# Key-value sums of a second attention layer as bursts on two column halves of the array, with a head-half layout and the last tile in halves

## The chip, the cores and the metric

The kernel runs on one core of a Trainium2 chip. The metric is the device time of the core in microseconds (us), from many executions; most of them agree within 0.3%. The profiled span of one execution is about 1.7 us shorter than its device time. All runs quoted are fast, at a granted TensorE clock of 0.995 to 1.000, unless the text says otherwise.

Ratios below are computed as the mean time of one kernel's fast runs over the mean time of the other kernel's fast runs of the same rounds, so they are not quite the ratio of the medians that stand beside them. The interval after a ratio is its 95% interval.

PE is TensorE, PEld its weight loads, DVE is VectorE, ACT is ScalarE, POOL is GpSimd, SP is SyncE. "num" means the numerator matmuls of the linear attention.

## The reference, cut to what matters

Four residual layers on 2048 tokens of width 512: linear attention with a learned feature map (A), gated ReLU unit (B), A again, B again, with the same weights both times.

```python
x = x + A(layernorm(x));  x = x + B(layernorm(x))
x = x + A(layernorm(x));  x = x + B(layernorm(x))

def A(x):                                   # 32 heads of width 16
    phi_q = [softmax(q @ w_phi), softmax(-q @ w_phi)]     # 2 x 16 features
    phi_k = [softmax(k @ w_phi), softmax(-k @ w_phi)]
    kv  = einsum("bhsf,bhsd->bhfd", phi_k, v)             # sum over all tokens
    z   = einsum("bhsf->bhf", phi_k)
    num = einsum("bhqf,bhfd->bhqd", phi_q, kv)
    den = einsum("bhqf,bhf->bhq", phi_q, z) + 1e-6
    return (num / den) @ wo

def B(x):
    return (relu(x @ W_gate) * (x @ W_up)) @ W_down       # inner width 1376
```

The sum over all tokens matters here: no numerator of the second attention layer can start before the last token tile (tile 15 of 16, 128 tokens each) has gone through its layer normalisation, its key projection, its softmax and its key-value sum.

## The kernel before

The program is emitted as a graph of operations, each with an engine, the buffers it reads and writes, and a planned duration in ns. A list scheduler then decides the order of the instructions on each engine, and the engines run those orders with semaphore waits between them. It tries 4 weights and 12 passes and keeps the order with the shortest planned span. So a changed duration or dependency anywhere can move instructions everywhere.

The parts that the change and the argument touch:

```python
# layer normalisation of one token tile (the "apply" is the last line)
op("dve", bn_stats(stats6[t] <- x_sb[t]));  op("dve", bn_aggr(mv[t] <- stats6[t]))
op("pool", rv1 = var + eps);                op("pool", rstd = rv1 ** -0.5)
op("dve", tensor_scalar(ytile[yb] <- (x_sb[t] - mean) * rstd))    # 128x512 bf16, planned 407 ns
dma_transpose(yT[t] <- ytile[yb])                                  # on the SP queue

# key normalisation of one tile
op("dve", tensor_reduce(Zk <- expk[t]))                            # planned 1215
op("dve", reciprocal(rZk <- Zk))                                   # planned 545
parts = [("pool", 0, 2)] if t < NT - 2 else [("pool", 0, 1), ("dve", 1, 2)]
for eng, s0, s1 in parts:
    op(eng, tensor_tensor(expk[t, s0:s1] <- expk[t, s0:s1] * rZk)) # planned 1930 on GpSimd

def kv_acc(self, t, tag):                   # 8 matmuls of 128x129 for each token tile
    for g in range(NG):
        s, c = g // 4, g % 4
        bank, j = g // 3, g % 3
        op("pe", matmul(pb[bank][:, j * 130:j * 130 + 129],
                        expk[t, s, c * 128:(c + 1) * 128],         # stationary, 128 columns
                        vsb[t, c, 0:129]), ...)                    # moving, 8 heads x 16, and ones
# ... kv_fin: two products on VectorE for each of three banks build the masked kvbd ...

# the turn from layer 1 (B) to layer 2 (A)
mix(steps_B(tiles(3)), steps_K(1) + steps_K(2) + [lambda: self.q_proj(0, mring, "A2")])
for t in range(12):
    self.kv_acc(t, "A2")
for f in steps_K(3):
    f()
for t in tiles(3):
    self.kv_acc(t, "A2")
self.kv_fin("A2")

def glu_down(self, t, ring, tag):           # 11 matmuls of 128x512, one residual, later one store
```

The softmax here doesn't subtract the row's maximum and nothing guards it: scores larger than these inputs give would overflow.

## Time and profile before

| | before |
|---|---|
| device time, median of 3 first runs | 394.07 us |
| profiled span | 392.7 us |
| PE busy / DVE busy / ACT busy / POOL busy | 96% / 68% / 53% / 42% |
| first numerator of layer 1 / of layer 2 | 54.84 / 241.10 us |
| first gate matmul of the last layer | 259.11 us |

The page of the kernel before, its busy times and its chain that ended last (shares of the span by engine):

```profile
PE 377.3 (96%) x2277; PEld 206.9 (53%) x2320; DVE 267.4 (68%) x554; ACT 207.1 (53%) x389; POOL 166.4 (42%) x272
...
PE 84%; DVE 5%; POOL 4%; DMA 2%; ACT 2%; issue 2%; SPq 0%; DVEq 0%; ACTq 0%; POOLq 0%
```

TensorE is busy nearly always, and the chain runs mostly along it. The next view is the chain between 216 and 245 us, which is the turn to layer 2; its first line gives shares by line of the program (L587 key and value projection, L633 key-value sums, L660 query projection, L752 down projection of layer 1).

```profile
by line: PE ps L587 31.8%; PE ps L633 20.8%; PE ps L660 19.9%; PE ps L752 17.0%; PE ps L676 5.3%; DVE kvbd L644 3.7%; DVE kvbd L649 0.8%; issue 0.8%
```

Here the chain is TensorE alone, down to the two VectorE products just before the numerators. The timeline of PE (start, duration, engine, line, operands, count, and in brackets the idle time before the group and what ended it):

```profile
236.16 1.36 PE L633 MATMUL ps<-vsb,expk 128*128 128x129 bf16 x21
237.36 1.03 PE L587 MATMUL ps<-wv_p,yT 128*128 128x512 bf16 x4
238.22 2.82 PE L633 MATMUL ps<-vsb,expk 128*128 128x129 bf16 x46
241.10 0.54 PE L676 MATMUL ps<-kvbd,expq 128*128 128x144 bf16 x6
```

The last 46 sums are a backlog: (2.82 - 0.22) / 45 = 58 ns each, without a hole. No bracket stands on any of these lines. GpSimd's last key product of tile 15 ended at 239.24. The line of that product in the kernel before:

```profile
237.74 1.50 POOL L604 TENSOR_TENSOR expk<-expk,rZk 128x512 bf16<-128x512 bf16 x1 [0.94 <-DVE rZk L601]
```

One more view of the kernel before is needed later: VectorE's layer-norm applies of tiles 12 to 15 of layer 2.

```profile
216.50 0.41 DVE L564 TENSOR_SCALAR ytile<-x_sb,mv,rstd 128x512 bf16<-128x512 bf16 x1
221.17 1.75 DVE L564 TENSOR_SCALAR ytile<-x_sb,mv,rstd 128x512 bf16<-128x512 bf16 x1
224.84 0.41 DVE L564 TENSOR_SCALAR ytile<-x_sb,mv,rstd 128x512 bf16<-128x512 bf16 x1
227.13 0.41 DVE L564 TENSOR_SCALAR ytile<-x_sb,mv,rstd 128x512 bf16<-128x512 bf16 x1 [1.06 <-POOL rstd L552]
```

The same instruction takes 0.41 us three times and 1.75 us once.

### The profile page before, as it was taken

Reading aid. Unit: us, or ns where it says so; the run is one execution under the profiler, and the core shown is the slowest. Engines: PE = TensorE matmul, PEld = TensorE weight load, DVE = VectorE, ACT = ScalarE, POOL = GpSimd, SP = SyncE. Lnnn points to the kernel's source line nnn. Section 1 sums busy time; section 2 is a strip of 40 time slices with the busy share of each in tenths; the row PEclk is TensorE's granted clock in tenths of the full one; section 3 lists DMA queues with packets and bytes.
Section 4 is the critical chain, followed back from the end, with each engine's and each line's share of the span. In section 5 each row is a group of like instructions: output and inputs, shape, how many; then the busy total and the mean of one; then the engine's idle time right before and its main releaser. Section 6 shows DMA issues by size and latency. Waiting matters only on the chain.

```text
span 392.7 us, 6311 instructions
## 1 busy us (share of the span) xinstructions
PE 377.3 (96%) x2277; PEld 206.9 (53%) x2320; DVE 267.4 (68%) x554; ACT 207.1 (53%) x389; POOL 166.4 (42%) x272
## 2 busy tenths in 40 slices
PE   5889999999999999999999999989999999999996
PEld 3445564677644444444444467467774454444442
DVE  4999878777757899857747867877875666222122
ACT  5898659744624413532553484975564462453350
POOL 5389945642623463363334552574444253000000
PEclk9999999999999999999999999999999999999999
DMA  6833672322211322401000110242323132100001
GB/s 182 220 69 79 200 276 43 67 53 43 42 40 27 43 53 46 85 7 29 13 13 2 27 29 2 48 61 53 76 54 61 27 56 53 42 14 13 15 27 53
DMA packets 61519, 23.01 MB, mean 59 GB/s; under 512 B 53456, under 2 KB 60464, under 8 KB 61488
## 3 DMA queue, kind: packets, MB, share of 16 engines
q1 hardware_dynamic: 60912, 22.08, 24.8%
q10 hardware_dynamic: 576, 0.52, 0.5%
q8 instruction: 18, 0.29, 0.3%
q14 instruction: 13, 0.11, 0.1%
HBM read 7.91 MB, written 2.10 MB: 25 GB/s over the span
## 4 chain that ended last, share of the span: by engine, by line
PE 84%; DVE 5%; POOL 4%; DMA 2%; ACT 2%; issue 2%; SPq 0%; DVEq 0%; ACTq 0%; POOLq 0%
PE ps L728 39%; PE ps L752 19%; PE ps L587 7%; PE ps L707 6%; PE ps L660 5%; PE ps L676 4%; POOL expk L604 3%; DVE stats L547 2%; PE ps L633 2%; PE ps L618 2%; DMA yT<-ytile 1%; DMA x_sb<-in_A_x_dram 1%; POOL rstd L552 1%; DVE ytile L564 1%; ACT expq L663 1%
## 5 line engine op out<-in xcount | busy, mean ns | idle before, releaser
L728 PE MATMUL ps<-yT,Wg 128*128 128x512 bf16 (+3 forms) x435 | 125.9, 336 | 2.0 <-ACT numbf L366 1.1
L728 PE MATMUL ps<-yT,Wu 128*128 128x512 bf16 (+3 forms) x436 | 124.2, 336 | 0.4
L730 ACT ACTIVATE gate_sb<-ps 128x512 bf16<-128x512 f32 (+3 forms) x110 | 56.2, 512 | 108.7 <-PE ps L728 103.2
L752 PE MATMUL ps<-Wd,hT 128*128 128x512 bf16 (+1 forms) x340 | 104.0, 379 | 0.6
L604 POOL TENSOR_TENSOR expk<-expk,rZk 128x1024 bf16<-128x1024 bf16 (+1 forms) x32 | 59.6, 1878 | 30.9 <-DVE rZk L601 21.6
L728 PEld LDWEIGHTS ps<-yT,Wg 128*128 128x128 bf16 (+1 forms) x440 | 43.7, 100 | 34.4 <-issue 1.5
L728 PEld LDWEIGHTS ps<-yT,Wu 128*128 128x128 bf16 (+1 forms) x440 | 43.7, 100 | 33.4 <-ACT expk L735 0.8
L752 PEld LDWEIGHTS ps<-Wd,hT 128*128 128x128 bf16 (+1 forms) x352 | 34.1, 98 | 37.3 <-DVE x_sb L754 0.7
L737 DVE TENSOR_TENSOR hT<-gate_sb,expk 128x512 bf16<-128x512 bf16 (+3 forms) x73 | 28.7, 393 | 31.0 <-ACT expk L735 30.2
L547 DVE BATCH_NORM_STATS2 stats<-x_sb 128x6 f32<-128x512 bf16 x64 | 42.1, 675 | 5.0 <-DMA x_sb<-in_A_x_dram 4.7
L599 DVE TENSOR_REDUCE Zk<-expk 128x64 f32<-128x1024 bf16 x32 | 38.0, 1197 | 10.1 <-ACT expk L590 8.4
L366 ACT ACTIVATE numbf<-ps 128x432 bf16<-128x432 f32 x64 | 32.9, 538 | 17.7 <-PE ps L676 17.4
L701 POOL TENSOR_TENSOR osb<-tsc 128x512 bf16<-128x512 bf16 x28 | 32.7, 1168 | 21.3 <-DVE tsc L696 18.2
L707 PE MATMUL ps<-wo_p,oT 128*128 128x512 bf16 x122 | 38.7, 379 | 0.2
L551 POOL TENSOR_SCALAR rv<-mv 128x1 f32<-128x1 f32 (+1 forms) x55 | 12.3, 229 | 61.0 <-DVE mv L548 60.8
L735 ACT ACTIVATE expk<-ps 128x512 bf16<-128x512 f32 (+3 forms) x73 | 36.2, 495 | 0.6 <-PE ps L728 0.4
L754 DVE TENSOR_TENSOR x_sb<-x_sb,ps 128x512 bf16<-128x512 bf16 x32 | 21.7, 682 | 20.8 <-PE ps L752 20.6
L663 ACT ACTIVATE expq<-ps 128x1024 bf16<-128x1024 f32 (+1 forms) x40 | 32.3, 865 | 6.1 <-PE ps L660 5.8
L676 PE MATMUL ps<-kvbd,expq 128*128 128x144 bf16 x256 | 34.6, 226 | 0.4 <-DVE kvbd L649 0.2
L660 PE MATMUL ps<-yT,Wqp 128*128 128x512 bf16 x121 | 33.6, 379 | 1.2 <-ACT expq L663 1.0
L740 DVE TENSOR_TENSOR hT<-gate_sb,ps 128x512 bf16<-128x512 bf16 (+2 forms) x37 | 22.6, 612 | 17.7 <-PE ps L728 15.7
L552 POOL TENSOR_TENSOR rstd<-rv,mhalf 128x1 f32<-128x1 f32 (+1 forms) x55 | 33.1, 607 | 3.1
(62 smaller groups left out, 428.9 us busy)
## 6 DMA issues: line engine op xcount, KB each, us to landing
out_dram<-x_sb SPq DMA_DIRECT2D x16, 128.0 KB, 1.7
x_sb<-in_A_x_dram SPq DMA_DIRECT2D x3, 512.0 KB, 6.2
Wg<-in_B_W_gate_dram SPq DMA_DIRECT2D x4, 344.0 KB, 4.2
Wu<-in_B_W_up_dram SPq DMA_DIRECT2D x4, 344.0 KB, 6.6
Wd<-in_B_W_down_dram SPq DMA_DIRECT2D x5, 256.0 KB, 7.3
yT<-ytile SPq DMA_TRANSPOSE x60, 2.4
hT<-in_A_wqkv_dram ACTq DMA_DIRECT2D x4, 128.0 KB, 3.2
x_sb<-in_A_x_dram SPq DMA_DIRECT2D x4, 128.0 KB, 3.8
```

Of the source, the lines that this page charges most:

```text
L547: op("dve", (lambda t: lambda e: e.bn_stats(k.stats6[:, t, :], k.x_sb[:, t, :]))(t), [r("x", t)], [r("st", t)], 685, f"{tag} stats {t}")
L552: op("pool", lambda e: e.tensor_tensor(k.rstd[:, t0:t1, :], k.rv1[:, t0:t1, :], k.mhalf[:, 0:n], ALU.pow), [r("rv1", t) for t in ts] + [r( ...
L599: op("dve", lambda e: e.tensor_reduce(k.Zk[:, zb, :], k.expk[:, t, :, :].rearrange("p s (h f) -> p (s h) f", f=16), AX.X, ALU.add), [r("ex ...
L604: op(eng, (lambda s0, s1: lambda e: e.tensor_tensor(k.expk[:, t, s0:s1, :].rearrange("p s (h f) -> p (s h) f", f=16), k.expk[:, t, s0:s1, ...
L660: op("pe", (lambda c, ic, bank: lambda e: e.matmul(k.pb[bank][:], k.Wqp[:, ic, c * 128:(c + 1) * 128], k.yT[:, ic, st * 512:(st + 1) * 512 ...
L663: op("act", (lambda c0, s, b0: lambda e: e.activation(k.expq[:, st, c0:c0 + w, s, :], k.ps[:, b0:b0 + w, :], ACT.Exp, scale=(1.0 - 2.0 * s ...
L676: op("pe", (lambda s, c, j, g0, bank: lambda e: e.matmul(k.pb[bank][:, j * GW:(j + 1) * GW], k.expq[:, st, c, s, tt * 128:(tt + 1) * 128], ...
L707: op("pe", (lambda c, bank: lambda e: e.matmul(k.pb[bank][:], k.oT[:, ob, c, :], k.wo_p[:, c, :], start=(c == 0), stop=(c == NC - 1)))(c, ...
L728: op("pe", (lambda bank, W, ic, fc, Mf: lambda e: e.matmul(k.pb[bank][0:Mf, 0:n], W[:, ic, fc * 128:fc * 128 + Mf], k.yT[:, ic, c0:c0 + n] ...
L730: op("act", (lambda Mf, gb, gs: lambda e: e.activation(k.gate_sb[0:Mf, gs, 0:n], k.pb[gb][0:Mf, 0:n], ACT.Relu))(Mf, gb, gs), [self.RP[gb] ...
L735: op("act", (lambda Mf, ub, tu: lambda e: e.activation(k.expk[0:Mf, tu, 0, 0:n], k.pb[ub][0:Mf, 0:n], ACT.Copy))(Mf, ub, tu), [self.RP[ub] ...
L752: op("pe", (lambda fc, Kf, u, c0: lambda e: e.matmul(k.pb[bank][:], k.hT[0:Kf, u, c0:c0 + 128], k.Wd[0:Kf, fc, :], start=(fc == 0), stop=( ...
```

## The change

Its intent is to save TensorE time. Of each 128x128 product of the sums only the blocks where key head and value head agree are used. Splitting the 8 heads of a group into two halves of 4 lets each matmul hold 64 stationary columns and move 65 columns (64 values and ones), and the two halves sit on two column halves of the array, where they can run side by side. To change the array's mode seldom, the sums of several tiles are one uninterruptible operation (4, 4, 4, 3 and 1 tiles). The layout of `vsb`, `kvbd`, `wo_p` and the numerators follows the head halves. Layer 1 keeps full-width sums. The last tile's down projection, residual and store go in two column halves on two queues.

```diff
-GW = 144
+GH = 72
+GW = 2 * GH
-        sb("vsb", [NT, NC, 130])
+        sb("vsb", [NT, NC, 2, 66])
-        sb("kvbd", [NG, GW])
+        sb("kvbd", [NG, 2, GH])
 ... layouts of wo_p, numbf, tsc, zm, ab follow the halves ...
+    def kv_burst(self, ts, tag):
+        def acc(e):
+            for t in ts:
+                for s in range(2):
+                    for c in range(NC):
+                        for u in range(2):
+                            last = e.matmul(
+                                k.pb[s][u * 64:u * 64 + 64, c * 65:c * 65 + 65],
+                                k.expk[:, t, s, c * 128 + u * 64:c * 128 + u * 64 + 64],
+                                k.vsb[:, t, c, u, 0:65], start=..., stop=...)
+            return last
+        self.op("pe", acc, [all phik and v of ts], self.RP[0:2], 190 + 256 * len(ts), ...)
+    def kv_burst_fin(self, tag):   # four 128x256 products, one add (zt), one product (kvden)
 ...
-                mix(steps_B(tiles(3)), steps_K(1) + steps_K(2) + [lambda: self.q_proj(0, mring, "A2")])
-                for t in range(12):
-                    self.kv_acc(t, "A2")
+                mix(steps_B(tiles(3)), steps_K(1) + steps_K(2))
+                for ts in [[0, 1, 2, 3], [4, 5, 6, 7], [8, 9, 10, 11]]:
+                    self.kv_burst(ts, "A2")
                 for f in steps_K(3):
                     f()
-                for t in tiles(3):
-                    self.kv_acc(t, "A2")
-                self.kv_fin("A2")
+                self.q_proj(0, cycle([2, 3]), "A2", w=2)
+                for ts in [[12, 13, 14], [15]]:
+                    self.kv_burst(ts, "A2")
+                self.kv_burst_fin("A2")
 ... glu_down(..., halves) and store(..., halves): 2 for the last tile of the last layer
```

## The prediction

> **What bounds the kernel now.** TensorE. The page's busy table gives PE 96% of a 392.7 us span at granted clock 1.0 (next: VectorE, 68%). The chain of waits gives PE 84%. At the turn from layer 1 to layer 2 the stretch table shows PE busy 16.89 of 17.00 us (224 to 241 us) and 17.42 of 18.00 us (241 to 259), so there time is worth what PE work is worth.
>
> **What the change removes.** Layer 2's key-value sums are 128 matmuls of 128x129. In the timeline 46 of them in a row take 2.82 us with a 0.22 us tail: 58 ns each, so about 7.4 us of PE time for the layer. They become 256 matmuls with 64 stationary columns and 65 moving columns, in five bursts (the built order shows 64, 64, 64, 48, 16). One moving pass of 65 instead of 129 columns, two halves side by side, would need about 65/129 of 58 ns = 29 to 32 ns per pair: 16 ns a matmul, 4.1 us in all (estimate). "TensorEngine Tiling (Array Packing)" in the Trainium skill says under Key Properties that tiles run in parallel and that changing the mode drains the array, and under Restrictions that column tiling disables fast weight load. This trace has hints only of the last: a 96-column weight load takes 123 ns, a 128-column one 98. I put entry and exit at 0.2 us a burst (about the 0.22 us matmul latency), 1 us together. So PE work falls by about 2.3 us if halves overlap fully, by nothing if weights set the pace at about 27 ns a matmul, and grows if the halves don't overlap.
>
> **What it adds.** (1) The sums of tile 15 go as one burst, and everything behind waits for its end: four 4x64 products on VectorE (about 0.42 us each, as the 128x256 form now takes 0.424), one add (0.17), one product (0.2): 2.2 us to the first numerator matmul. Before, the first two bank products ran under the last sums, and the timeline shows no hole before the numerators. The built order puts 6 query matmuls (1.3 us) into this gap: about 0.9 us idle is left. (2) Before, the sums were a backlog that hid the key-normalisation chain (exp 1.1, reduce 1.2, reciprocal 0.55, product up to 1.5 us); with less backlog PE should wait for tile 15's product, some 0.5 us. (3) Query exponentials go in pairs: 4.2 instead of 4.8 us of ScalarE, nearly free.
>
> **Tail.** Last residual 256 wide (0.41 instead of 0.69 us), last store halved on two queues (landing 1.7 us now): minus 0.3 to 0.5 us.
>
> The head-half layout leaves other element counts alone; I expect the 0.68 us scaling product (VectorE) unchanged. The order of layer 1's sums is unchanged; the scheduler reshuffles much of the middle, worth plus or minus 0.7 us.
>
> **Sum.** PE work -2.3 (sure of this at about 60%), new holes +1.2 to +1.5, tail -0.4: about 1.3 us less, 392.8 us. Range 390.8 to 395.2. Chances: faster by over 2%: 0.01; within 2%: 0.98; slower: 0.01.
>
> **What would show it.** Groups: about 16 ns spacing in the key-value sums of layer 2, each burst of 64 in 1.1 to 1.3 us. Timeline: a hole of about 0.5 us before the last one or two bursts, released by GpSimd's or VectorE's product, and about 0.9 us before the first numerators, released by VectorE's last kvbd product. End: last store starts about 0.3 us after the last residual's shorter run. Scaling product still 0.68 us.
>
> **What would make it wrong.** Weight loads that pace the halves (27 ns or more a matmul: sums 7 us or more, time about 394 to 395); drains much over 0.2 us; a 4-element inner run that slows VectorE's or GpSimd's products; a schedule that happens to be better or worse elsewhere.

## The result, and the profile after

| | before | after |
|---|---|---|
| device time, median (4 runs each) | 394.23 us | 394.91 us |
| lowest to highest | 393.86 to 394.43 | 394.30 to 395.15 |
| ratio after / before | | 1.0016 (0.9999 to 1.0033) |
| profiled span | 392.7 us | 393.3 us |

The change made the kernel neither faster nor slower by 2%. It is probably some 0.6 us slower (the interval just takes in no difference at all), where 1.3 us less had been predicted.

The time can be split at three marks that every profile has. Apart from the sums and the last tile's halves, both kernels do the same TensorE operations between these marks, by the built order, except that one query matmul (0.22 us) lies on the other side of the second mark.

| stretch | before | after | difference |
|---|---|---|---|
| start to first numerator of layer 1 | 54.84 | 55.21 | +0.37 |
| to first numerator of layer 2 | 186.26 | 186.64 | +0.38 |
| to first gate matmul of the last layer | 18.01 | 19.27 | +1.26 |
| to the end of the span | 133.6 | 132.2 | -1.4 |
| span | 392.7 | 393.3 | +0.6 |

The first difference is noise: five profiles with the order of the kernel before start their numerators at 54.74 to 55.08, five with the order of the kernel after at 54.44 to 55.30. The second stretch should have lost 2.3 us and gained 0.4. The third gained 1.3 where nothing had been expected. The fourth gave most of that back.

The page after:

```profile
PE 379.2 (96%) x2459; PEld 204.6 (52%) x2459; DVE 272.5 (69%) x555; ACT 206.2 (52%) x385; POOL 167.5 (43%) x273
...
PE 77%; DVE 11%; POOL 4%; DMA 4%; issue 2%; ACT 1%; SPq 0%; POOLq 0%; DVEq 0%
```

The busy time of PE is no measure of the saving, because some matmul records are missing from the profile before (2277 of a count that should be 139 below the 2459 after). But the chain has moved: PE's share fell from 84% to 77% and DVE's rose from 5% to 11%. The same 216 to 245 us of the chain as above (L604 key sums, L569 layer-norm applies, L606 reciprocals, all on VectorE):

```profile
by line: DVE Zk L604 23.3%; DVE ytile L569 18.0%; DVE rZk L606 9.6%; PE ps L700 9.5%; issue 7.4%; POOL expk L609 5.2%; DVE kvbd L682 4.9%; PE ps L795 4.5%; DVE stats L552 4.2%; PE ps L716 3.6%; DVE x_sb L797 2.7%; PE ps L592 2.2%; POOL rstd
```

The chain that was TensorE alone is now VectorE's: layer norm and key normalisation of the last tiles. The bursts themselves are what was predicted. The timeline of PE, bursts only, and the two lines after them:

```profile
222.99 1.20 PE L669 MATMUL ps<-vsb,expk 128*64 128x65 bf16 x64
...
225.95 1.20 PE L669 MATMUL ps<-vsb,expk 128*64 128x65 bf16 x64
...
234.40 1.20 PE L669 MATMUL ps<-vsb,expk 128*64 128x65 bf16 x64
...
236.94 0.95 PE L669 MATMUL ps<-vsb,expk 128*64 128x65 bf16 x48 [0.37 <-POOL expk L609]
...
239.38 0.44 PE L669 MATMUL ps<-vsb,expk 128*64 128x65 bf16 x16 [0.52 <-POOL expk L609]
...
241.41 0.60 PE L700 MATMUL ps<-yT,Wqp 128*128 128x512 bf16 x2 [0.61 <-DVE zt L687]
241.85 0.54 PE L716 MATMUL ps<-kvbd,expq 128*128 128x144 bf16 x6
```

64 matmuls take 1.20 us; less a latency of 0.195 that is 16 ns each. The five stretches add up to 4.99 us, against about 7.4 us before. So the array did run the halves side by side (a pair of halves takes 32 ns; one full-width sum of 65 columns takes 30 ns in an experiment below). Entering and leaving the two-half mode shows in the starts of the matmuls: behind a 512-column matmul the next one usually starts after 0.216 us; the first of each of the first three bursts comes 0.09 us later than that, and the matmul behind each of the five bursts 0.11 us later than the 16 ns spacing. That is 0.2 us a burst, 1.0 us in all, so 256 x 16 ns = 4.1 us and 1.0 us stand against 7.4 us: TensorE has some 2.3 us less to do.

The brackets show the new waits, 0.37 + 0.52 us for GpSimd's key products and 0.61 us for `zt`. They count from the end of the matmul before, which the profile models: 0.38 us after its start for 512 columns, although the next one can start after 0.216 us. Counted from start to start, these holes are 0.53, 0.69 and 0.78 us, and a fourth, which waits for a transpose at 232.13, is 0.29 us: 2.3 us in all, or 2.1 us without the entry into two bursts. Tile 15's key product on GpSimd starts at 237.74 and ends at 239.23, where before it ended at 239.24: although TensorE has less to do, the last product isn't ready any earlier.

```profile
237.74 1.49 POOL L609 TENSOR_TENSOR expk<-expk,rZk 128x512 bf16<-128x512 bf16 x1 [0.95 <-DVE rZk L606]
```

The chain's VectorE instructions after, the layer-norm applies of tiles 13 to 15, and GpSimd's key products next to them. First VectorE's:

```profile
218.51 1.60 DVE L569 TENSOR_SCALAR ytile<-x_sb,mv,rstd 128x512 bf16<-128x512 bf16 x1
...
223.09 1.76 DVE L569 TENSOR_SCALAR ytile<-x_sb,mv,rstd 128x512 bf16<-128x512 bf16 x1
...
227.72 1.94 DVE L569 TENSOR_SCALAR ytile<-x_sb,mv,rstd 128x512 bf16<-128x512 bf16 x1 [0.56 <-POOL rstd L557]
```

Then GpSimd's, from the same timeline of the kernel after:

```profile
218.04 1.93 POOL L609 TENSOR_TENSOR expk<-expk,rZk 128x1024 bf16<-128x1024 bf16 x1
...
222.77 1.93 POOL L609 TENSOR_TENSOR expk<-expk,rZk 128x1024 bf16<-128x1024 bf16 x1 [0.89 <-DVE rZk L606]
...
227.58 1.93 POOL L609 TENSOR_TENSOR expk<-expk,rZk 128x1024 bf16<-128x1024 bf16 x1
```

Add start and duration: the products end at 219.97, 224.70 and 229.51, the applies at 220.11, 224.85 and 229.66. Each of these three applies starts inside a GpSimd product and ends 0.14 to 0.15 us after it, whenever it began. Alone it takes 0.41 us. The Trainium skill says why, in "SBUF — State Buffer", section "Who interferes with whom": VectorE in its two-port modes, which `tensor_scalar` can enter, and GpSimd share a port pair, and "Whoever issues first gets the shared pair for the whole instruction; the other fully blocks". The trace agrees with the page. In the kernel before only one of these applies met a product (221.17 for 1.75 us); after the change all three of tiles 13, 14 and 15 do, and together they lose 1.60 + 1.76 + 1.94 - 3 x 0.41 = 4.1 us of VectorE (1.3 us before), on the very chain that ends in tile 15's sum.

In the third stretch the same happens once more. Tile 0's layer-norm apply of the last layer, in the kernel after:

```profile
254.82 1.16 DVE L569 TENSOR_SCALAR ytile<-x_sb,mv,rstd 128x512 bf16<-128x512 bf16 x1
```

GpSimd's output sum runs from 254.68 to 255.83 there. Before, that apply and tile 1's took 0.96 us together, from 254.87.

The end of the kernel shows the halves. Before, the timeline from 386 us, with the last residual and the last two stores:

```profile
389.54 1.20 SPq L759 DMA_DIRECT2D out_dram<-x_sb  x2
389.69 0.69 DVE L754 TENSOR_TENSOR x_sb<-x_sb,ps 128x512 bf16<-128x512 bf16 x1 [0.18 <-PE ps L752]
```

And after:

```profile
390.43 0.86 DVE L797 TENSOR_TENSOR x_sb<-x_sb,ps 128x256 bf16<-128x256 bf16 x2 [1.28 <-PE ps L795]
391.32 0.35 ACTq L804 DMA_DIRECT2D out_dram<-x_sb  x1
```

From the end of the last matmul (389.66 before, 390.83 after) to the end of the span it was 3.0 us and is 2.5 us: about 0.5 us gained. Another 0.8 to 0.9 us of the fourth stretch is a wait of the kernel before just ahead of 264.17 us. PE's bracket there says 1.09 us and names an eviction of ScalarE, but the record of one output matmul is missing at that place. Its weight load is there, and it waited for the transpose of an output tile:

```profile
263.94 0.10 PEld L707 LDWEIGHTS ps<-wo_p,oT 128*128 128x128 bf16 x1 [1.15 <-DMA oT<-osb]
```

Two later profiles of the same order that lack no record show the matmul itself, waiting 0.77 and 0.81 us for that transpose. The kernel after has such a wait too, but earlier, in the third stretch (0.82 us at 259.77). This is not a part of the change but of how the scheduler laid the instructions.

### The profile page after: what moved, and what is told of

Same layout as the page of the kernel before. It is cut to its first block, busy times and chain, and to the rows that moved or that the text cites. A ratio compares the mean times of both kernels' runs of the same rounds, so it can differ in the third digit from the quotient of the medians.

```text
span 393.3 us, 6628 instructions
## 1 busy us (share of the span) xinstructions
PE 379.2 (96%) x2459; PEld 204.6 (52%) x2459; DVE 272.5 (69%) x555; ACT 206.2 (52%) x385; POOL 167.5 (43%) x273
## 4 chain that ended last, share of the span: by engine, by line
PE 77%; DVE 11%; POOL 4%; DMA 4%; issue 2%; ACT 1%; SPq 0%; POOLq 0%; DVEq 0%
PE ps L768 37%; PE ps L795 19%; PE ps L747 6%; PE ps L592 5%; PE ps L700 4%; PE ps L716 4%; POOL expk L609 3%; DVE ytile L569 2%; DVE Zk L604 2%; DVE stats L552 2%; DMA oT<-osb 2%; PE ps L623 2%; DVE rZk L606 1%; DMA x_sb<-in_A_x_dram 1%; DMA yT<-ytile 1%
## 5 line engine op out<-in xcount | busy, mean ns | idle before, releaser
L768 PE MATMUL ps<-yT,Wg 128*128 128x512 bf16 (+3 forms) x440 | 127.6, 336 | 0.8 <-DMA yT<-ytile 0.4
L770 ACT ACTIVATE gate_sb<-ps 128x512 bf16<-128x512 f32 (+3 forms) x110 | 56.2, 512 | 111.6 <-PE ps L768 102.6
L795 PE MATMUL ps<-Wd,hT 128*128 128x512 bf16 (+2 forms) x363 | 105.2, 373 | 0.0
L795 PEld LDWEIGHTS ps<-Wd,hT 128*128 128x128 bf16 (+1 forms) x363 | 35.2, 98 | 36.1 <-DVE x_sb L797 0.4
L777 DVE TENSOR_TENSOR hT<-gate_sb,expk 128x512 bf16<-128x512 bf16 (+3 forms) x73 | 29.9, 410 | 31.0 <-ACT expk L775 30.1
L604 DVE TENSOR_REDUCE Zk<-expk 128x64 f32<-128x1024 bf16 x32 | 37.9, 1193 | 9.3 <-ACT expk L595 7.4
L747 PE MATMUL ps<-wo_p,oT 128*128 128x512 bf16 x128 | 40.8, 379 | 1.2 <-DMA oT<-osb 1.1
L797 DVE TENSOR_TENSOR x_sb<-x_sb,ps 128x512 bf16<-128x512 bf16 (+1 forms) x33 | 22.0, 667 | 23.5 <-PE ps L795 23.1
L700 PE MATMUL ps<-yT,Wqp 128*128 128x512 bf16 x128 | 34.9, 380 | 1.5 <-ACT expq L703 0.9
L569 DVE TENSOR_SCALAR ytile<-x_sb,mv,rstd 128x512 bf16<-128x512 bf16 x58 | 31.3, 544 | 6.6 <-POOL rstd L557 6.1
L595 ACT ACTIVATE expk<-ps 128x512 bf16<-128x512 f32 x44 | 23.9, 597 | 21.0 <-PE ps L592 20.8
```

Source lines behind the costliest of these rows:

```text
L569: op("dve", lambda e: e.tensor_scalar(k.ytile[:, yb, :], k.x_sb[:, t, :], k.mv[:, t, 0:1], k.rstd[:, t, :], op0=ALU.subtract, op1=ALU.mult ...
L604: op("dve", lambda e: e.tensor_reduce(k.Zk[:, zb, :], k.expk[:, t, :, :].rearrange("p s (h f) -> p (s h) f", f=16), AX.X, ALU.add), [r("ex ...
L700: op("pe", (lambda c, ic, bank: lambda e: e.matmul(k.pb[bank][:], k.Wqp[:, ic, c * 128:(c + 1) * 128], k.yT[:, ic, st * 512:(st + 1) * 512 ...
L747: op("pe", (lambda c, bank: lambda e: e.matmul(k.pb[bank][:], k.oT[:, ob, c, :], k.wo_p[:, c, :], start=(c == 0), stop=(c == NC - 1)))(c, ...
L768: op("pe", (lambda bank, W, ic, fc, Mf: lambda e: e.matmul(k.pb[bank][0:Mf, 0:n], W[:, ic, fc * 128:fc * 128 + Mf], k.yT[:, ic, c0:c0 + n] ...
L770: op("act", (lambda Mf, gb, gs: lambda e: e.activation(k.gate_sb[0:Mf, gs, 0:n], k.pb[gb][0:Mf, 0:n], ACT.Relu))(Mf, gb, gs), [self.RP[gb] ...
```

## The experiments

Four theories stood at the start. Theory 1: the chain of tile 15 through VectorE and GpSimd sets the start of the numerators, so that TensorE time saved there becomes waiting. In its sharper form, 1b, it is the layer-norm applies, blocked by GpSimd's products, that make that chain late. Theory 2: it is TensorE work after all, and bursts cost more than they save (entering the mode, for example). Theory 3: the head-half layout, with 4 elements in the inner run instead of 8, slows the products. Theory 4: the scheduler's re-ordering elsewhere decides.

All runs were correct unless said otherwise. In the first call the kernel before took 394.37 us (median of 11), in the second 394.46 (9), in the third 394.45 (10), in the fourth 394.47 (9).

### The layout alone

```diff
 # the changed kernel, but layer 2's sums as in layer 1, query projection back in its old place, no halves
-                for ts in [[0, 1, 2, 3], [4, 5, 6, 7], [8, 9, 10, 11]]:
-                    self.kv_burst(ts, "A2")
+                for t in range(12):
+                    self.kv_acc(t, "A2")
```

> The head-half layout alone, layer 2's sums and query projections as before, no halved tail; the built order is nearly that of the kernel before. Theory 1 (tile 15's chain sets when the numerators start, so the time saved on TensorE turns into waits): layout free, ratio to before 1.000, within 0.1%, scaling product still 0.68 us. Theory 3 (the layout slows the products of the numerator stage): at least +0.4 us (+0.1%), the 32 scaling products or the 28 GpSimd products longer.

Measured: 393.98 us, ratio 0.9988 (0.9966 to 1.0011). One of its six executions took 2282.47 us; it is left out of the ratio. It was the profiled one: TensorE's matmuls took several times as long throughout, so this trace has no usable times of stages. The durations of VectorE and GpSimd can still be read in it. The 32 scaling products take 684 ns (median) and the 28 output sums on GpSimd 1.15 us, as in the kernel before (682 ns, 1.15 us). The layout costs nothing that five timed runs can show, and the products that theory 3 names are no longer: theory 3 falls. The same trace shows one thing more. With TensorE so slow, no apply runs into a GpSimd product, and none of the 58 applies on VectorE takes more than 0.54 us.

### The tail alone, and what the scheduler made of it

```diff
 # the kernel before, with glu_down(..., halves) and store(..., halves) of the change
-        216, f"{tag} down {t} {fc}")          # planned duration of a down matmul
+        0.42 * w + 1, f"{tag} down {t} {fc}") # 216.04 for the full width
```

> The kernel before with the last tile's down projection, residual and store in two halves, nothing else. All theories: 0.3 to 0.5 us shorter at the end (ratio about 0.999). If it is nothing or longer, the tail is one of the places where the change lost what was predicted.

Measured: 396.59 us, ratio 1.0052 (1.0028 to 1.0076), 0.5% slower. In the profile the tail is not to blame: layer 1 is. The planned durations of all down matmuls and residuals differ by 0.04 ns, and the last tile has new operations; that was enough for another order to win the search. In layer 1, 350 us away from the tail, an apply ran into GpSimd's products. VectorE's and then GpSimd's lines of this run between 39 and 43 us:

```profile
40.14 2.10 DVE L564 TENSOR_SCALAR ytile<-x_sb,mv,rstd 128x512 bf16<-128x512 bf16 x1
```

```profile
38.28 3.81 POOL L604 TENSOR_TENSOR expk<-expk,rZk 128x1024 bf16<-128x1024 bf16 x2
```

Later, TensorE waited 2.1 us for a key product, and the first numerators of layer 1 started at 57.9 instead of 54.84 us (whether this apply alone made that wait was not tested):

```profile
55.19 1.22 PE L633 MATMUL ps<-vsb,expk 128*128 128x129 bf16 x16 [2.06 <-POOL expk L604]
56.20 1.91 PE L660 MATMUL ps<-yT,Wqp 128*128 128x512 bf16 x4
```

Not all of the 3 us is the wait. Between 56 and 60 us this profile has a granted clock of 0.57 instead of 1.00, and four query matmuls take 1.91 us instead of 1.03. Four of the six executions ran at a mean clock of 0.996, as this one (396.36 to 396.96 us); the two at 1.000 took 394.51 and 395.69 us. So a good part of the 0.5% comes with the lower clock, and what the order alone costs is open. Theory 4 is real as a size all the same: an edit that does nothing to layer 1 cost it 3 us in this profile. From then on the instruction order was frozen: the graph was scheduled as it stood, then emitted again with the edit, and each operation got the place of its namesake.

### Half the TensorE work in the sums of the kernel before

```diff
-                k.pb[bank][:, j * 130:j * 130 + 129], k.expk[...], k.vsb[:, t, c, 0:129],
+                k.pb[bank][:, j * 130 + 64:j * 130 + 129], k.expk[...], k.vsb[:, t, c, 64:129],   # layer 2 only
```

The result is wrong; the order is unchanged.

> The kernel before with only 65 instead of 129 moving columns in layer 2's sums (wrong result on purpose), instruction order the same: some 128 x 27 ns = 3.4 us less TensorE work, nothing else changed. Theory 2 (TensorE work sets the time here, and the change lost its saving to the cost of entering and leaving bursts): the time falls by 2.5 to 3.4 us. Theory 1: it falls by no more than about 1.8 us, because the last normalised keys landed 1.8 us before the numerators started, and the rest turns into a wait for GpSimd's product.

Measured: 393.83 us, ratio 0.9990 (0.9969 to 1.0010). The sums took 30 ns instead of 58 each, so layer 2 had 128 x 28 ns = 3.6 us less TensorE work, and the kernel gained about 0.4 us. The timeline of PE shows where the rest went:

```profile
239.10 0.95 PE L633 MATMUL ps<-vsb,expk 128*128 128x65 bf16 x26 [1.19 <-POOL expk L604]
239.88 0.38 PE L660 MATMUL ps<-yT,Wqp 128*128 128x512 bf16 x1
240.56 0.55 PE L676 MATMUL ps<-kvbd,expq 128*128 128x144 bf16 x6 [0.30 <-DVE kvbd L649]
```

A backlog that was full has become two holes, the larger for tile 15's key product. From the first numerator of layer 1 to that of layer 2 it is 185.76 us instead of 186.26 (186.26 and 186.64 in two later profiles of the unnarrowed order). So already in the kernel before, a second chain ran only some 0.5 to 0.9 us behind TensorE, and no saving in these sums alone could bring more. This supports theory 1.

### More TensorE work in the bursts of the changed kernel

```diff
-                        for u in range(2):
-                            last = e.matmul(k.pb[s][u * 64:u * 64 + 64, ...], k.expk[... 64 columns], k.vsb[:, t, c, u, 0:65], ...)
+                        last = e.matmul(k.pb[s][:, c * 128:c * 128 + 128], k.expk[... 128 columns], k.vsb[:, t, c, :, 0:64], ...)
```

Full-width matmuls, half as many, in the same order and without a change of mode; wrong.

> The changed kernel with its bursts on the whole array: 128 stationary and 128 moving columns, half as many matmuls (wrong result on purpose: no denominators), same order. About 64 x 2 x 57 ns = 7.3 us in place of some 5 us, so +2.2 us of TensorE work. Theory 2: time rises by 2 us or more, or, if entering and leaving the split mode is what costs, by clearly less with the idle time ahead of each burst gone. Theory 1: the added work mostly fills the holes ahead of the last bursts, time rises by under 1 us.

Measured: 395.62 us, ratio 1.0041 (1.0019 to 1.0063). The five stretches of sums took 1.98 x 3 + 1.52 + 0.62 = 8.08 us instead of 4.99, 3.1 us more. No mode is entered, and the extra spacing before and behind a burst is gone: it is 0.002 us at most, where the two-half bursts have 0.09 and 0.11 us. So those 0.2 us a burst belong to the two-half form, and the net addition is 3.1 - 1.0 = 2.1 us. The stretch to the first numerator grew from 186.64 to 187.53 us, 0.9 us. So TensorE work in the bursts is worth less than half of its size there, and the two-half bursts are the better form: theory 2 falls.

### The applies of the last three tiles on ScalarE, order frozen

```diff
-                    self.ln(t, "L2")
+                    self.ln(t, "L2", on_act=self.mod and t >= 13)    # ScalarE activation, one extra small GpSimd scalar
+            # frozen: every other operation keeps the place that it has in the changed kernel
```

> The changed kernel with its instruction order frozen as it is, except that the three layer-norm applies of layer 2's token tiles 13, 14 and 15 (128x512, on VectorE) run on ScalarE, which is partly idle there. No work is removed. Theory 1b (VectorE's applies lose up to 1.5 us each while GpSimd multiplies a key tile, on the very chain that ends in the last key product): no apply of those three takes over 1 us, tile 15's last key product ends earlier than 239.2 us, the first numerator starts 0.7 to 1.5 us earlier than 241.85, and the time falls by 0.4 to 1.3 us against the changed kernel (ratio to before 0.998 to 1.000). Rival (the chain is set by something else, such as GpSimd's own queue or ScalarE's exponentials): the applies get short but the last key product still ends within 0.3 us of 239.2, first numerator within 0.3 us of 241.85, time unchanged at ratio 1.001 to 1.002.

Measured: 394.07 us, ratio 0.9991 (0.9971 to 1.0010). Against the changed kernel's ratio of 1.0016 that is 0.25%, about 1.0 us; the two intervals overlap, so the profile has to carry this. The applies take 0.80 us each on ScalarE, though GpSimd multiplies at the same time; the same section of the Trainium skill says that ScalarE never waits for those ports, and the trace agrees. Tile 15's last key product ends at 237.65 instead of 239.23, the two holes before the last bursts are gone, and the first numerator starts at 240.62 instead of 241.85:

```profile
218.97 0.80 ACT L566 ACTIVATE ytile<-x_sb,nmr,rstd 128x512 bf16<-128x512 bf16 x1
...
236.15 1.50 POOL L609 TENSOR_TENSOR expk<-expk,rZk 128x512 bf16<-128x512 bf16 x1 [0.94 <-DVE rZk L606]
...
240.62 0.54 PE L716 MATMUL ps<-kvbd,expq 128*128 128x144 bf16 x6
```

The chain from 216 to 245 us is TensorE's again:

```profile
by line: PE ps L592 41.2%; PE ps L700 21.1%; PE ps L669 16.1%; PE ps L795 11.9%; DVE kvbd L682 4.9%; PE ps L716 4.1%; DVE numbf L367 1.6%; issue 0.3%; DVE zt L687 0.3%
```

The stretch to the numerators is 185.32 us instead of 186.64, and two later runs with the same move repeat it (185.70 and 185.25). So it is shown that these three applies on VectorE held the chain up. The move takes from VectorE the 4.1 us of blocking and also the 3 x 0.41 us that the applies take anyway; this run does not separate the two. That the blocking is the larger part is read from the sizes. The third stretch stayed at 19.27 us, to the hundredth.

### The tail in halves, order frozen

```diff
+ glu_down(t, ..., halves=2) and store(t, halves=2) for the last tile, all else in the order of the kernel before
```

> The kernel before with its exact instruction order frozen, and only the last token tile's final down projection, residual and store in two column halves, as the change has them. It repeats the failed isolation of the tail without letting the scheduler re-order anything. If the tail in halves is worth what the two profiles suggest (last matmul to end of span 3.0 us before, 2.4 us after): 0.4 to 0.7 us faster than before, ratio 0.998 to 0.999. If the tail gains nothing and the shorter end in the changed kernel was luck of the DMA: ratio 1.000 within 0.0005. If the halves themselves made the earlier attempt slow: ratio 1.003 to 1.005 again.

Measured: 394.42 us, ratio 0.9998 (0.9979 to 1.0018): nothing gained. From the last matmul to the end of the span it did take 2.5 us instead of 3.0, but PE lost time just before that:

```profile
389.34 1.38 PE L755 MATMUL ps<-Wd,hT 128*128 128x256 bf16 x11 [0.34 <-DVE x_sb L757]
```

The second half's matmuls had to wait for a residual of an earlier tile that still read their PSUM bank.

### The second half in a bank of its own

```diff
-            bank = next(ring)
+            bank = next(ring) if m == 0 else 6
```

> As the earlier frozen run of the tail in halves, but the second half accumulates in an eighth-part of PSUM that is free by then (bank 6) instead of the bank that tile 14's residual was still reading; in that earlier run TensorE waited 0.34 us for that residual. If that wait is what took back the gain: last matmul to end of span about 2.5 us, as there, no wait before the second half, and 0.4 to 0.7 us faster than before, ratio 0.998 to 0.999. If the tail in halves is worth nothing in any case: ratio 0.9995 to 1.0005.

Measured: 394.23 us, ratio 0.9989 (0.9971 to 1.0007). The wait is gone, the last matmul ends at 389.84 and the span at 392.3, so the end takes 2.5 us instead of 3.0. The profile shows a gain of 0.5 us at the end; the timed gain of 0.2 to 0.4 us is not told apart from nothing.

### A scheduler rule against the overlap

```diff
+  # layer-norm applies, SBUF products (DVE) and key and output products (GpSimd) exclude each other in the plan
+  if o.port:
+      t = max(t, lock[other[o.eng]]);  lock[o.eng] = t + o.dur
```

> The kernel before, unchanged in its operations, with one rule added to the scheduler: VectorE's layer-norm applies and its products may not be placed at the same time as GpSimd's key products and output products. It tells how much the stalls cost in the whole of the kernel before. Theory 1b: the applies' mean falls from 484 ns towards 430, layer-2 numerators start at or before 240.5 us, 2 to 4 us faster than before (ratio 0.990 to 0.995). Rival (stalls sit where something else is waited for anyway): ratio 0.998 to 1.002.

> The changed kernel with the same rule in its scheduler as in the run before this one. Theory 1b, and that the change's saving of PE time was only hidden by the stalls: 3 to 5 us faster than before (ratio 0.988 to 0.993) and faster than the kernel before with that rule by 1 to 2.5 us. Rival (the burst layout is worth nothing even without stalls): the same as the kernel before with that rule, within 0.6 us.

Measured: the kernel before with the rule 398.59 us, ratio 1.0106 (1.0085 to 1.0126); the changed kernel with the rule 396.48, ratio 1.0053 (1.0032 to 1.0074). Both are slower, against both theories' numbers. The rule did not do what it was for: the applies' mean, 484 ns before and 544 after the change, is 517 and 508 ns with it. Five applies of the kernel before took more than 0.48 us; with the rule nine do, and eight of these end 0.15 us after a GpSimd product, at other places. The rule holds in the plan; that the engines drift against the plan by more than an apply's length is the likely reason, and was not measured. Layer 1 also lost more than a microsecond (first numerator at 56.1 and 56.2 us). So these two runs say nothing for or against theory 1b. That the changed kernel gained 2.1 us over the kernel before here compares two entirely different orders, and nothing follows from it.

### The control: the same three applies on ScalarE in the kernel before

```diff
 # as the frozen run with the applies on ScalarE, from the kernel before
+                    self.ln(t, "L2", on_act=self.mod and t >= 13)
```

> The control for the run that moved three layer-norm applies to ScalarE: the same move (tiles 13, 14, 15 of layer 2) in the kernel before, its instruction order frozen otherwise. Of these three only one lost time there (221.17 for 1.75 us; the last two took 0.41 us), and a backlog of sums hides the chain behind them until 241.04 us. Theory 1b (in the changed kernel the stalls ate the saving; in the kernel before they cost little): within 0.5 us of the kernel before, ratio 0.9985 to 1.0005, first numerator at 240.6 to 241.2. Rival (moving the applies is simply good for any kernel, so it says nothing about the change): about 1 us faster, ratio 0.997 to 0.998, first numerator at 239.9 to 240.3.

Measured: 394.75 us, ratio 1.0012 (0.9993 to 1.0032), first numerator at 241.59. The ratio and the first numerator both lie a little outside what theory 1b allowed (1.0005 and 241.2), in the direction away from the rival. So moving the applies is not good for any kernel; it helped the changed one because there it removed a loss that the changed order had brought. Why the kernel before got a little slower, if it did, was not followed.

### Mending the third stretch, first try

Tile 1's chain (statistics, GpSimd scalars, apply, transpose) feeds the first gate matmul. Three edits in the frozen order:

```diff
 # on top of the run with three applies on ScalarE
+ VectorE: tile 0's apply one place earlier, ahead of GpSimd's output sum of tile 3
+ GpSimd:  rv1 and rstd of tile 1 ahead of zm and zd of tile 4
+ TensorE: the four output matmuls of tile 3 behind the first eight gate and up matmuls
```

> The run of the changed kernel with three applies on ScalarE, with three more small re-orderings in its frozen order and no other operation moved: tile 0's layer-norm apply of the last layer issues one instruction earlier on VectorE, ahead of GpSimd's output sum of tile 3 (it lost 0.76 us behind that sum, 253.58 for 1.17); tile 1's two GpSimd scalars go ahead of two small products of tile 4; and tile 3's four output matmuls, which waited 0.84 us for their transpose, go behind the first eight gate and up matmuls. Theory (the port stall of tile 0's apply delays tile 1's chain and with it the first gate matmul): that apply takes about 0.41 us, the first gate matmul starts at 258.9 to 259.3 instead of 259.89, and the time falls a further 0.5 to 1.0 us, to a ratio of 0.996 to 0.998 against before, which would be faster than both kernels. Rival (that stage is set by ScalarE's total work): first gate matmul or its first evictions no earlier, time unchanged at 0.999.

Measured: 395.23 us, ratio 1.0018 (0.9994 to 1.0042); three of its six runs came at a granted clock of 0.995 or 0.996 and took 395.92 to 396.23 us, the other three 394.04 to 394.54. The apply did shrink, but the gate matmuls did not move. VectorE's timeline:

```profile
253.15 0.41 DVE L569 TENSOR_SCALAR ytile<-x_sb,mv,rstd 128x512 bf16<-128x512 bf16 x1
...
256.34 0.35 DVE L731 RECIPROCAL zr<-zd 128x32 f32<-128x32 f32 x1 [1.60 <-POOL zd L730]
256.61 0.40 DVE L367 CAST numbf<-ps 128x288 bf16<-128x288 f32 x1
256.92 0.40 DVE L569 TENSOR_SCALAR ytile<-x_sb,mv,rstd 128x512 bf16<-128x512 bf16 x1
```

Tile 1's apply stands behind a reciprocal of tile 4, and that reciprocal now waits for the GpSimd scalars that the edit itself had put back: 1.60 us of idle. The first gate matmul started at 259.85, after 2.19 us of idle PE. So removing the block of tile 0's apply alone was worth nothing. What feeds the gate is tile 1's apply, and its place in VectorE's queue.

### Mending the third stretch, second try

```diff
 # on top of the run with three applies on ScalarE; TensorE's order untouched
+ VectorE: tile 0's apply one place earlier; tile 1's apply ahead of tile 4's reciprocal and a numerator copy
+ GpSimd:  rv1 and rstd of tile 1 ahead of zm and zd of tile 4
```

> The mended run before this one shortened tile 0's layer-norm apply to 0.41 us but its first gate matmul stayed at 259.85, because VectorE reached tile 1's apply (256.92) only behind a reciprocal of tile 4, which the same edit had made wait for GpSimd until 256.34. Here that apply goes ahead of the reciprocal and of one numerator copy, and TensorE's order is left as in the run with three applies on ScalarE; nothing else differs from that run. If tile 1's chain starts the gate matmuls: its apply starts at 255.7 to 256.0 instead of 256.63, the first gate matmul at 258.7 to 259.2 instead of 259.89, the span ends 0.4 to 1.0 us earlier than 392.3, ratio to before 0.9965 to 0.9985. If the start of the gate matmuls is earlier but the span is not: something behind it (ScalarE's evictions of that stage, or the output transposes) sets the pace, ratio 0.999 to 1.000.

Measured: 393.38 us (392.65 to 393.64), ratio 0.9977 (0.9962 to 0.9991). This is faster than the kernel before by a small margin, well within 2%, whose interval leaves out 1; with the changed kernel it was not timed in the same rounds (394.91 us there). VectorE's two applies and the first gate matmul:

```profile
252.28 0.41 DVE L569 TENSOR_SCALAR ytile<-x_sb,mv,rstd 128x512 bf16<-128x512 bf16 x1
...
254.94 0.41 DVE L569 TENSOR_SCALAR ytile<-x_sb,mv,rstd 128x512 bf16<-128x512 bf16 x1 [1.06 <-POOL rstd L557]
```

```profile
257.88 0.27 PE L768 MATMUL ps<-yT,Wg 128*128 128x256 bf16 x1 [0.23 <-issue]
```

This profile ran 0.3 to 0.9 us ahead of the others from layer 1 on (first numerator of layer 1 at 54.44), so the stretches are the fair comparison:

| profile | to first num of layer 2 | to first gate | to the end |
|---|---|---|---|
| before | 186.26 | 18.01 | 133.6 |
| before, half the sum work | 185.76 | 18.02 | 132.9 |
| before, tail in halves (frozen) | 186.64 | 18.01 | 133.5 |
| before, tail with own bank | 186.26 | 18.01 | 133.0 |
| before, applies on ScalarE | 186.85 | 18.08 | 133.2 |
| after | 186.64 | 19.27 | 132.2 |
| after, full-width bursts | 187.53 | 19.18 | 131.9 |
| after, applies on ScalarE | 185.32 | 19.27 | 132.4 |
| after, mended, first try | 185.70 | 19.29 | 132.8 |
| after, mended, second try | 185.25 | 18.19 | 133.0 |

The third stretch follows the order alone: 18.0 to 18.1 in five profiles, 19.2 to 19.3 in four, and 18.2 where tile 1's apply was put forward. That edit moved two VectorE and two GpSimd instructions. Part of its gain is lost again in the last stretch, where TensorE has a new wait of 1.15 us for an output transpose at 263.00.

## Why the prediction was right or wrong

The class (within 2%) and the range, 390.8 to 395.2, held. The direction did not: 1.3 us less was predicted, and the change is probably some 0.6 us slower. That the range held says little, since it is 4.4 us wide and the time lies 0.3 us below its upper end.

- **PE work -2.3 us: right.** 16 ns a matmul in bursts was the number predicted and measured, and a burst of 64 took 1.20 us. Weights did not set the pace. Entry and exit cost the 0.2 us a burst that was put in; that figure was a guess from the latency of a matmul, so its fit is luck.
- **Hole of 0.5 us before the last bursts, from GpSimd's product: right in kind, too small.** The brackets give 0.89 us (0.37 and 0.52); from start to start and without the entry into the mode it is 1.0 us. A hole of 0.29 us for a transpose was not foreseen.
- **Hole of 0.9 us before the numerators: right in kind, 0.61 us by the bracket, 0.78 us from start to start**, released by `zt`, one step later than named. All holes together are 2.1 us, where 1.4 us had been predicted.
- **Tail -0.3 to -0.5 us: right, 0.5 us** by the profile. Isolated, it is worth that only if the second half need not wait for its PSUM bank.
- **Layout free: right** (scaling product 682 and 684 ns; ratio 0.9988 for the layout alone).
- **Reshuffle of the middle, plus or minus 0.7 us: too small.** A new tail, with planned durations that differ by 0.04 ns elsewhere, moved the kernel by 0.5%, in layer 1, in part by a lower clock there. In the change itself the reshuffle put three applies under GpSimd products (worth 1.0 us, shown by moving them), put tile 1's apply late (1.1 us, shown by moving it forward with its GpSimd scalars), and took a wait of 0.8 to 0.9 us out of the last stretch (only read in the profile).

The step that failed is this one of the prediction: PE is busy 16.89 of 17.00 us and 17.42 of 18.00, "so there time is worth what PE work is worth". A full engine says that it is the longest chain, not by how much. Halving the sums in the kernel before, which took 3.6 us of TensorE work out and nothing else, gained 0.4 us: the chain of tile 15 through VectorE and GpSimd was only 0.5 to 0.9 us behind. With the applies on ScalarE, so that this chain is early enough, the stretch to the numerators is 185.25 to 185.70 us against 186.26 to 186.85 in the profiles of the kernel before without narrowed sums, 1.1 us by the means. So even then less than half of the 2.3 us arrives: the hole of 0.78 us before the numerators stays, and so does the query matmul of 0.22 us that moved in.

In the changed kernel the account of the stretch between the two first numerators closes with the holes counted from start to start: 2.3 us less work, 0.2 us for the query matmul that moved in, 2.1 us of holes, which makes 0.0. Measured is a growth of 0.4 us against the profile before, and between 0.0 and 0.4 us against three profiles of its order (186.26, 186.64, 186.26). So the whole saving went into these four holes. The remainder lies within what single profiles of one order differ by.

## What to carry to other kernels

Before saving work on a full engine, ask how far behind the second chain runs. An unbroken backlog hides that, and the cheapest way to measure it is to take the work out wrongly (narrower operands, same order) and see what the time does. Where a scheduler lays out everything, freeze the order before comparing parts of a change, or the comparison measures the scheduler. And read VectorE's groups by single durations, not by means: an instruction that takes 0.41 us alone and 1.9 us under a GpSimd instruction is a wait that no idle time shows.

## What the Trainium skill lacked or had wrong

- "SBUF — State Buffer", section "Who interferes with whom": right in every case looked at here, and short of one number that makes it easy to see in a profile. A blocked VectorE apply is recorded as one long busy instruction (1.60, 1.76, 1.94 us instead of 0.41) that ends 0.14 to 0.15 us after GpSimd's; the page has a delay behind the release for the opposite case alone. The idle columns show nothing of it.
- "TensorE: Matmul & The Clock Gate", section "Wait — 56ns, not 53.3ns?", says that start-to-start between matmuls never drops below about 25 ns, however small they are. Alternating between two 64-column halves with 65 moving columns, this trace shows 16 ns (64 in 1.20 us with 0.195 us latency). The floor there holds for one tile at most; for two halves the measurement decides.
- "TensorEngine Tiling (Array Packing)", sections "Key Properties" and "Restrictions": that column tiling turns fast weight load off fits the trace (64 columns load in 111 ns, 128 columns in 97), but no run here tells this from the mere width, since 96 columns without tiling take 123 ns. That changing the mode drains the array is stated without a figure; here entering the mode costs 0.09 us and leaving it 0.11 us from start to start, and full-width bursts at the same places cost 0.002 us at most.
- No page has the cost of planning for the port lock: a scheduler that excluded the overlaps by planned times left the applies at 517 and 508 ns on average, where they are 484 and 544 ns without it.
